# Tying the conversions of the later weight chunks to one another in VectorE's order

## The chip, the cores and the metric

The kernel runs on one core of a Trainium2 chip. The metric is the time of one execution in microseconds of the device; the kernel's time is the median of several executions. The core's engines named here are TensorE (PE in the rows; PEld is its weight load), VectorE (DVE), ScalarE (ACT), GpSimd (POOL) and SyncE (SP), which issues all of this kernel's DMAs. Each engine works through its own row of instructions in a fixed order; an instruction that waits for another engine or for a DMA holds up all behind it in its row.

## The reference

Windowed attention with a linear bias, followed by two feed-forward networks on the same 2304 tokens (4 x 576, 512 features as 8 heads of 64):

```python
scores = q @ k.T / sqrt(64) + slope[head] * -|i - j|   # only 0 <= i - j < 128
x = softmax(scores) @ v                                # 4 x 8 x 576 x 64 -> 2304 x 512
h = x @ w_in                                           # 512 -> 2048
x = (h * sigmoid(1.702 * h)) @ w_out                   # 2048 -> 512
g = x @ w_gate; val = x @ w_val                        # 512 -> 1536
out = (silu(g) * val) @ w_out2                         # 1536 -> 512
```

The inputs of the networks come as 64-bit floating-point words, which the kernel turns into pairs of 32-bit words itself.

## The kernel before

**Work.** The 2304 tokens are 18 tiles of 128, worked in five blocks of 4, 2, 4, 4 and 4 tiles (blocks 0 to 4). For each block attention makes the input x of the first network; the second network runs when all blocks are through the first. Every product of the first network is made as three matmuls, since each operand is a high and a low part: high x high (L554), high x low (L555), low x high (L556).

**Weights of the first network.** They come in 16 chunks. Chunk f is 128 of the 2048 hidden features: its part of w_in and its part of w_out, 512 KB each (`load_w`, L186). A chunk is converted in five steps (`split_steps`): L197 on ScalarE turns the upper words into a first value `cv`; L199 on VectorE shifts the lower words in place (`wraw`); L201 on VectorE puts both together in `cv`; L206 on ScalarE writes the high part of the weight `wt`; L208 on VectorE writes the low part. `cv` has two buffers, so two chunks can be under way. Chunks 0 to 7 are loaded at the start, 8 to 11 when the values of block 0 are made, 12 to 15 after that.

**Order.** The beginning is written out by hand: a table of tokens (`PLAN`) fixes the rows of TensorE, VectorE, ScalarE and GpSimd, with the attention of blocks 0 and 1 and the conversions of chunks 0 to 8 among it. Behind it a loop goes through pairs of block and chunk, `seq`: (0, 0..7), (1, 0..15), (0, 8..15), then (2, 0..15) and so on. For each pair `h_part` makes h = x @ w_in of the chunk, ScalarE and VectorE make its activation (th: L575 tanh on ScalarE, L577 on VectorE; gh: L583 on ScalarE; gl: L585 on VectorE), and two pairs later `y_part` multiplies it with w_out. Ahead of the products the loop calls `split_next` for the chunks that they need. In that part the rows of the engines are not fixed by hand: a scheduler places each instruction, by its own idea of when it can run, among the others, so that an instruction written late in the program can stand early in its engine's row.

**Attention.** Per pair of heads and tile: scores on TensorE (L354), masking (L317, L319, L324) and row minima (L379) on VectorE, exponentials and their sums on ScalarE (L395), reciprocals on VectorE (L407, L408), normalising on GpSimd (L414), transposes on TensorE (L446), values on TensorE (L507, L519), and the high and low parts of x, xh on ScalarE (L551) and xl on VectorE (L543).

**Names in the rows.** `wraw` is a raw chunk, `wt` a converted one, `sb` a bank of scores, `prob` and `stat` the probabilities and their row statistics, `hp` the bank of h, `y` that of the output, `wg` a weight tile of the second network. In the rows of the order the tiles have numbers: wraw_138 is chunk 2, 147 chunk 5, 548 to 557 chunks 8 to 11, 1044 chunk 13, 1050 chunk 15; wt_789 is chunk 4, wt_1037 chunk 8 and wt_1169 chunk 9.

Of the kernel before, what the change touches and what calls it, by code (L numbers as in the profile page):

```python
# [8 lines left out]
F32 = mybir.dt.float32  # L9
# [4 lines left out]
ALU = mybir.AluOpType  # L14
# [72 lines left out]
def attention_two_ffn(ctx: ExitStack, tc: tile.TileContext, q, k, v, w_in, w_out, w_gate, w_val, w_out2, yscr, wscr, woscr, out):  # L87
# [5 lines left out]
    nc = tc.nc  # L93
# [95 lines left out]
    def split_steps(raw):  # L189


        words, pool, tag = raw
        low, high = words[:, :, :, 0], words[:, :, :, 1]
        c = cvp.tile([P, 2, 512], U32, tag="cv", name="cv")
        cf = c.bitcast(F32)

        nc.scalar.activation(out=cf, in_=high.bitcast(F32), func=AF.Prelu, scale=REBIAS, alpha=NEGATIVE)  # L197
        yield
        nc.vector.tensor_scalar(out=low, in0=low, scalar1=29, scalar2=None, op0=ALU.logical_shift_right)  # L199
        yield  # L200
        nc.vector.scalar_tensor_tensor(  # L201
            out=c, in0=c, scalar=3, in1=low, op0=ALU.logical_shift_left, op1=ALU.bitwise_or
        )
        yield
        t = pool.tile([P, 2, 2, 512], F32R, tag=tag, name="wt")
        nc.scalar.activation(out=t[:, :, 0, :], in_=cf, func=AF.Copy)  # L206
        yield
        nc.vector.tensor_tensor(out=t[:, :, 1, :], in0=cf, in1=t[:, :, 0, :].bitcast(F32), op=ALU.subtract)  # L208
        yield [t[:, 0], t[:, 1]]

    def w1_src(i):
# [347 lines left out]
    marks = {}  # L559
# [292 lines left out]

    def split_next(w, raw, upto):
        for i in range(len(w), min(len(raw), upto)):
            w[i] = list(split_steps(raw[i]))[-1]

    for hp in range(H // 2):
        load_full(hp)
# [6 lines left out]
    def step(token):  # L865
# [10 lines left out]
        elif op == "N":  # L876
            reciprocals(*at)
        elif op == "P":
            normalise(*at)
        elif op == "T":  # L880
            transposes(*at, int(fills or 0))
        elif op in "CL":
            if op == "C" or at[0] or 2 * at[1] + at[2] not in ON_VECTOR:
                apart(*at, op == "L")
        elif op == "V":
            values(*at)
            valued[at[0]] += 1
            if at[0] == 1 and valued[1] <= H // 2 - 2:
                load_pair(1, valued[1] + 1)
            if at[0] == 0 and valued[0] == H // 2:  # L890
                load_w1(4)
        elif op in "XZ":
            take_x(*at, op == "Z")
        elif op in "Habcd":
            if op == "H":
                parts[at] = h_steps(*at)
            next(parts[at])
        elif op == "Y":
            y_part(*at)
        else:  # L900
            if op == "w0":
                splits[at] = split_steps(raw1[at[0]])
            done = next(splits[at])
            if op == "w4":
                w1[at[0]] = done
# [106 lines left out]
    for idx, (j, f) in enumerate(seq):  # L1012
# [4 lines left out]
        if j < 2:  # L1017
            need = f + 2
            if j == 1:
                need = max(need, F0 + (NF1 - F0) * (f + 1) // NF1)  # L1020
            split_next(w1, raw1, need)
# [109 lines left out]
```

## Time and profile before

| | us |
|---|---|
| runs | 931.45, 934.69, 935.67 (median 934.69) |
| the profiled execution, all of it | 936.22 |
| its span in the trace | 934.3 |
| TensorE busy | 904.1 |
| VectorE busy | 676.8 |
| ScalarE busy | 452.2 |
| GpSimd busy | 117.3 |

The span is from the first to the last recorded instruction; the execution has 1.9 us around it. The mean granted clock of TensorE is 0.989 of full speed. The rows further down are from this one execution. Such a row begins with the start and the duration; "[6.13 <-DMA ...]" at its end is the time for which the engine had stood idle before it, and what ended that.

### The profile page before, as it was taken

The page shows a single profiled execution, that of the slowest core. Times are in us where ns is not written, and L with a number is a line of the kernel's source. Part 1 is how long each engine was busy: PE and PEld are TensorE (multiplying, and loading weights), DVE is VectorE, ACT ScalarE, POOL GpSimd, SP SyncE. Part 2 cuts the span into 40 slices and gives each one's busy share as a digit, 9 for nine tenths or more (in the row PEclk, how much of TensorE's full clock was granted, in tenths as well). Part 3 has the DMA queues.
Part 4 walks back from the last instruction along what each step waited for, and adds up shares of the span by engine and source line. Part 5 has one row for each costly group of instructions (what it writes and reads, how often), then busy time and mean ns, then how long its engine had stood idle before and what let it go on. Part 6 is the DMA issues. An engine that isn't in the chain of part 4 may idle for free.

```text
span 934.3 us, 15603 instructions
## 1 busy us (share of the span) xinstructions
PE 904.1 (97%) x5572; PEld 801.1 (86%) x5572; DVE 676.8 (72%) x1716; ACT 452.2 (48%) x1052; POOL 117.3 (13%) x221
## 2 busy tenths in 40 slices
PE   6779999999999999999999999999999999999998
PEld 4456898777777877778888899999999999999998
DVE  7668685676676667766647668899976679866777
ACT  5645474554465446554434445545444435344331
POOL 4632102331233003230000000000000000000000
PEclk9979999999999999999999999999999999999999
DMA  9943311344654445434563587999897667887763
GB/s 327 343 178 105 119 47 34 115 159 140 217 196 161 155 173 186 139 125 174 201 234 114 214 325 282 319 351 340 323 342 283 247 238 242 281 298 249 262 243 136
DMA packets 72461, 201.30 MB, mean 215 GB/s; under 512 B 6848, under 2 KB 38080, under 8 KB 65472
## 3 DMA queue, kind: packets, MB, share of 16 engines
q1 hardware_dynamic: 72384, 200.31, 60.3%
q8 instruction: 44, 0.72, 0.3%
q14 instruction: 33, 0.27, 0.1%
HBM read 156.76 MB, written 43.52 MB: 214 GB/s over the span
## 4 chain that ended last, share of the span: by engine, by line
PE 87%; DMA 8%; DVE 2%; SPq 1%; ACT 1%; issue 0%; POOL 0%; DVEq 0%; ACTq 0%
PE sx L705 15%; PE ox L705 8%; PE sz L705 8%; PE hp L554 7%; PE y L554 7%; PE hp L556 7%; PE hp L555 7%; PE y L555 7%; PE y L556 6%; PE sy L705 4%; PE oz L705 4%; DMA wraw<-in_moe_w_out 4%; PE xb L507 2%; PE sb L354 2%; PE oy L705 2%; PE pt L446 1%
## 5 line engine op out<-in xcount | busy, mean ns | idle before, releaser
L705 PE MATMUL sx<-ya,wg 128*128 128x384 f32 x864 | 172.2, 336 | 1.2 <-DMA wg<-w_scratch 1.0
L705 PEld LDWEIGHTS sx<-ya,wg 128*128 128x128 f32 x864 | 151.6, 188 | 2.1 <-DMA wg<-w_scratch 2.0
L554 PE MATMUL hp<-xh,wt 128*128 128x512 f32 (+1 forms) x320 | 122.2, 382 | 1.5 <-DVE stat L379 1.4
L556 PE MATMUL hp<-xh,wt 128*128 128x512 f32 (+1 forms) x320 | 119.7, 374 | 0.3 <-DVE wt L208 0.3
L555 PE MATMUL hp<-xl,wt 128*128 128x512 f32 (+1 forms) x320 | 119.6, 374 | 0.0
L555 PE MATMUL y<-gl,wt 128*128 128x512 f32 (+1 forms) x320 | 117.9, 372 | 0.0
L556 PE MATMUL y<-gh,wt 128*128 128x512 f32 (+1 forms) x320 | 117.4, 371 | 0.0
L554 PE MATMUL y<-gh,wt 128*128 128x512 f32 (+1 forms) x320 | 113.6, 378 | 1.2 <-DVE yt L618 0.6
L414 POOL TENSOR_SCALAR prob<-prob,stat 128x128 f32<-128x128 f32 x144 | 67.6, 488 | 214.4 <-DVE stat L408 129.1
L585 DVE TENSOR_TENSOR gl<-th,gh 128x512 fp32r<-128x512 f32 (+1 forms) x80 | 51.9, 648 | 57.7 <-ACT gh L583 56.8
L705 PE MATMUL ox<-p,wg 128*128 128x384 f32 x432 | 89.7, 337 | 0.7 <-DMA wg<-wo_scratch 0.7
L705 PE MATMUL sz<-ya,wg 128*128 128x384 f32 x432 | 88.0, 336 | 0.0
L734 DVE TENSOR_TENSOR p<-th,p 128x384 fp32r<-128x384 f32 x126 | 68.2, 553 | 25.0 <-ACT p L733 24.2
L583 ACT ACTIVATE gh<-th 128x512 fp32r<-128x512 f32 (+1 forms) x80 | 46.8, 585 | 72.2 <-PE y L556 58.5
L733 ACT ACTIVATE p<-th 128x384 fp32r<-128x384 f32 x126 | 63.7, 521 | 35.1 <-DVE th L729 24.9
L705 PEld LDWEIGHTS ox<-p,wg 128*128 128x128 f32 x432 | 76.5, 188 | 1.0 <-DMA wg<-wo_scratch 1.0
L705 PEld LDWEIGHTS sz<-ya,wg 128*128 128x128 f32 x432 | 76.0, 188 | 0.1
L395 ACT ACTIVATE prob<-prob,stat 128x128 f32<-128x128 f32 x144 | 56.2, 392 | 39.4 <-DVE stat L379 39.4
L554 PEld LDWEIGHTS hp<-xh,wt 128*128 128x128 f32 x320 | 61.3, 192 | 14.5 <-issue 3.1
L556 PEld LDWEIGHTS hp<-xh,wt 128*128 128x128 f32 x320 | 61.3, 192 | 11.7 <-DVE wt L208 0.8
L554 PEld LDWEIGHTS y<-gh,wt 128*128 128x128 f32 x320 | 58.1, 188 | 15.0 <-issue 1.8
L555 PEld LDWEIGHTS hp<-xl,wt 128*128 128x128 f32 x320 | 61.4, 192 | 9.9
(94 smaller groups left out, 1535.9 us busy)
## 6 DMA issues: line engine op xcount, KB each, us to landing
wg<-w_scratch SPq DMA_DIRECT2D x36, 1024.0 KB, 5.2
wg<-w_scratch SPq DMA_DIRECT2D x36, 768.0 KB, 6.4
wg<-wo_scratch SPq DMA_DIRECT2D x18, 1024.0 KB, 6.4
wg<-wo_scratch SPq DMA_DIRECT2D x18, 768.0 KB, 8.1
w_scratch<-wa SPq DMA_DIRECT2D x24, 512.0 KB, 2.7
w_scratch<-wb SPq DMA_DIRECT2D x24, 384.0 KB, 3.2
wraw<-in_moe_w_in SPq DMA_DIRECT2D x16, 512.0 KB, 8.5
wraw<-in_moe_w_out SPq DMA_DIRECT2D x16, 512.0 KB, 8.8
```

What stands on the lines that cost most here:

```text
L354: nc.tensor.matmul(out=sb[e][c : c + size, (i % 2) * 256 + lo : (i % 2) * 256 + hi], lhsT=u["q"][rows, i * P + c : i * P + c + size], rhs= ...
L395: nc.scalar.activation(out=prob[:, x], in_=prob[:, x], func=AF.Exp, bias=stat[:, 0, x : x + 1], scale=-1.0, accum_out=stat[:, 1, x : x + 1],)
L414: (nc.vector if (j, hp, g) in NORM_ON_VECTOR else nc.gpsimd).tensor_scalar(out=prob[:, x], in0=prob[:, x], scalar1=stat[:, 3, x : x + 1], ...
L507: nc.tensor.matmul(out=x[r][e * D : (e + 1) * D, i * P + a : i * P + a + w], lhsT=u["v"][e][keys, kt + lead, :], rhs=u["pf"][keys].rearran ...
L554: nc.tensor.matmul(out=out_ap, lhsT=whi, rhs=xhi, start=start, stop=False)
L555: nc.tensor.matmul(out=out_ap, lhsT=whi, rhs=xlo, start=False, stop=False)
L556: nc.tensor.matmul(out=out_ap, lhsT=wlo, rhs=xhi, start=False, stop=stop)
L583: a = nc.scalar.activation(out=gh[:, :m], in_=th[:, :m], func=AF.Copy)
L585: d = nc.vector.tensor_tensor(out=gl[:, :m], in0=th[:, :m], in1=gh[:, :m].bitcast(F32), op=ALU.subtract)
L705: nc.tensor.matmul(out=bank_[:, :HT], lhsT=w[:, kk, at, a, :], rhs=p2[2 * (q // 2 - 1) + kk, i][:, b, :] if m == "O" else y2[q // NP2, i][ ...
L733: nc.scalar.activation(out=t[:, 0], in_=src, func=AF.Copy)
L734: nc.vector.tensor_tensor(out=t[:, 1], in0=src, in1=t[:, 0].bitcast(F32), op=ALU.subtract)
```

## The change

The low-part instruction L208 of each conversion is remembered as `marks["w"]`. In `split_next` a chunk's conversion is now built under `tc.issue_after(marks["w"])`: on VectorE, the engine of the marked instruction, the steps of this chunk come behind L208 of the chunk before it. ScalarE's order is not tied. No wait is added; only places in VectorE's row change, and with them what the scheduler puts around them. Chunks 0 to 8 in the table are as they were. In the changed kernel lines behind L208 have numbers higher by 2.

```diff
-        nc.vector.tensor_tensor(out=t[:, :, 1, :], in0=cf, in1=t[:, :, 0, :].bitcast(F32), op=ALU.subtract)
+        marks["w"] = nc.vector.tensor_tensor(
+            out=t[:, :, 1, :], in0=cf, in1=t[:, :, 0, :].bitcast(F32), op=ALU.subtract
+        ).ins
         yield [t[:, 0], t[:, 1]]
...
     def split_next(w, raw, upto):
         for i in range(len(w), min(len(raw), upto)):
-            w[i] = list(split_steps(raw[i]))[-1]
+            with tc.issue_after(marks["w"]):
+                w[i] = list(split_steps(raw[i]))[-1]
```

First place: VectorE's row before, where the last reciprocals of block 0 (stat_497) stand among conversions; wraw_138 and wraw_147 belong to the table.

```order
L199 TENSOR_SCALAR wraw_138<-wraw_138 128x1024
L199 TENSOR_SCALAR wraw_551<-wraw_551 128x1024
L407 TENSOR_SCALAR stat_497<-stat_497 128x4
L408 RECIPROCAL stat_497<-stat_497 128x4
L543 TENSOR_TENSOR xl_370<-xb_527,xh_369 128x512
L201 SCALAR_TENSOR_TENSOR cv_468<-cv_468,wraw_138 128x1024
L199 TENSOR_SCALAR wraw_147<-wraw_147 128x1024
L543 TENSOR_TENSOR xl_370<-xb_539,xh_369 128x512
L199 TENSOR_SCALAR wraw_557<-wraw_557 128x1024
L317 MEMSET sb_569 64x128
```

The same piece of VectorE's row now:

```order
L199 TENSOR_SCALAR wraw_138<-wraw_138 128x1024
L409 TENSOR_SCALAR stat_497<-stat_497 128x4
L410 RECIPROCAL stat_497<-stat_497 128x4
L545 TENSOR_TENSOR xl_370<-xb_527,xh_369 128x512
L201 SCALAR_TENSOR_TENSOR cv_468<-cv_468,wraw_138 128x1024
L199 TENSOR_SCALAR wraw_147<-wraw_147 128x1024
L545 TENSOR_TENSOR xl_370<-xb_539,xh_369 128x512
L319 MEMSET sb_569 64x128
```

The shifts of chunks 9 (wraw_551) and 11 (wraw_557) have gone from there to places further down.

Second place: VectorE's row before, where a score tile of block 1 (sb_764) is masked and its minima are taken, ahead of the low part of chunk 4.

```order
L324 COPY_PREDICATED sb_764<-later_72,sb_764 64x2x64
L199 TENSOR_SCALAR wraw_1044<-wraw_1044 128x1024
L379 ISA prob_791,stat_792<-sb_764,bias_71 128x128
L379 ISA stat_792 128x1
L379 ISA prob_791,stat_792<-sb_764,bias_71 128x128
L379 ISA stat_792 128x1
L208 TENSOR_TENSOR wt_789<-cv_690,wt_789 128x2x512
```

The same piece of VectorE's row now:

```order
L326 COPY_PREDICATED sb_764<-later_72,sb_764 64x2x64
L381 ISA prob_791,stat_792<-sb_764,bias_71 128x128
L381 ISA stat_792 128x1
L381 ISA prob_791,stat_792<-sb_764,bias_71 128x128
L381 ISA stat_792 128x1
L208 TENSOR_TENSOR wt_789<-cv_690,wt_789 128x2x512
```

The shift of chunk 13 (wraw_1044) has gone from between the mask and the minima.

Third place: VectorE's row before, at the first activations of block 1 (th_1066, th_1098), where steps of chunks 8, 9, 10 and 15 stand mixed.

```order
L199 TENSOR_SCALAR wraw_1050<-wraw_1050 128x1024
L201 SCALAR_TENSOR_TENSOR cv_1165<-cv_1165,wraw_551 128x1024
L585 TENSOR_TENSOR gl_1032<-th_1025,gh_1031 128x512
L199 TENSOR_SCALAR wraw_548<-wraw_548 128x1024
L577 SCALAR_TENSOR_TENSOR th_1066<-th_1066,hp_1053 128x256
L208 TENSOR_TENSOR wt_1169<-cv_1165,wt_1169 128x2x512
L201 SCALAR_TENSOR_TENSOR cv_1027<-cv_1027,wraw_548 128x1024
L577 SCALAR_TENSOR_TENSOR th_1098<-th_1098,hp_1085 128x256
L585 TENSOR_TENSOR gl_1070<-th_1066,gh_1069 128x256
L201 SCALAR_TENSOR_TENSOR cv_1236<-cv_1236,wraw_554 128x1024
L624 TENSOR_SCALAR yt_1117<-y_705 128x512
L208 TENSOR_TENSOR wt_1037<-cv_1027,wt_1037 128x2x512
```

The same piece of VectorE's row now:

```order
L199 TENSOR_SCALAR wraw_548<-wraw_548 128x1024
L579 SCALAR_TENSOR_TENSOR th_1066<-th_1066,hp_1053 128x256
L579 SCALAR_TENSOR_TENSOR th_1098<-th_1098,hp_1085 128x256
L201 SCALAR_TENSOR_TENSOR cv_1027<-cv_1027,wraw_548 128x1024
L587 TENSOR_TENSOR gl_1070<-th_1066,gh_1069 128x256
L208 TENSOR_TENSOR wt_1037<-cv_1027,wt_1037 128x2x512
L199 TENSOR_SCALAR wraw_551<-wraw_551 128x1024
L626 TENSOR_SCALAR yt_1117<-y_705 128x512
L201 SCALAR_TENSOR_TENSOR cv_1165<-cv_1165,wraw_551 128x1024
L587 TENSOR_TENSOR gl_1102<-th_1098,gh_1101 128x256
L579 SCALAR_TENSOR_TENSOR th_1142<-th_1142,hp_1129 128x256
L208 TENSOR_TENSOR wt_1169<-cv_1165,wt_1169 128x2x512
```

Chunk 8 is finished before chunk 9 begins, and so on to chunk 15, with th and gl of block 1 between the steps.

## Rows read from the trace of the kernel before

**Rows 1.** The page: busy time of the engines, and the chain that ended last

```profile
PE 904.1 (97%) x5572; PEld 801.1 (86%) x5572; DVE 676.8 (72%) x1716; ACT 452.2 (48%) x1052; POOL 117.3 (13%) x221
PE 87%; DMA 8%; DVE 2%; SPq 1%; ACT 1%; issue 0%; POOL 0%; DVEq 0%; ACTq 0%
```

**Rows 2.** TensorE's waits: us in total, times, longest us

```profile
PE pt L446 <- POOL prob L414: 8.7, 4, 6.5
...
PE sx L705 <- DMA wg<-w_scratch: 1.0, 1, 1.0
```

**Rows 3.** Windows: length, busy us of each engine (instructions), clock, DMA share, GB/s

```profile
56.00:72.00 16.00, 16.00 (x72) 12.58 (x72) 12.34 (x27) 9.96 (x20) 5.63 (x8) 0.88 0.23 79
...
90.00:107.00 17.00, 17.00 (x91) 13.14 (x91) 9.81 (x14) 5.73 (x9) 5.51 (x7) 1.00 0.30 106
107.00:136.00 29.00, 28.94 (x218) 27.69 (x217) 27.28 (x38) 23.66 (x36) 0.00 (x0) 1.00 0.19 71
136.00:180.00 44.00, 44.00 (x408) 38.14 (x409) 26.93 (x119) 22.60 (x78) 12.50 (x28) 1.00 0.17 54
```

**Rows 4.** What VectorE waited for ahead of L199: us, times

```profile
  DMA wraw<-in_moe_w_out: 13.4, 4
```

**Rows 5.** VectorE's timeline, 49 to 52 us

```profile
49.95 0.70 DVE L199 TENSOR_SCALAR wraw<-wraw 128x1024 uint32<-128x1024 uint32 x1 [6.13 <-DMA wraw<-in_moe_w_out]
50.56 0.16 DVE L407 TENSOR_SCALAR stat<-stat 128x4 f32<-128x4 f32 x1
...
51.43 1.22 DVE L201 SCALAR_TENSOR_TENSOR cv<-cv,wraw 128x1024 uint32<-128x1024 uint32 x1
```

**Rows 6.** Timelines of ScalarE and GpSimd, 43 to 53 us

```profile
43.72 0.19 ACT L395 ACTIVATION_READ_ACCUMULATOR prob<-prob,stat 128x1 f32 x1
...
52.68 1.06 ACT L206 ACTIVATE wt<-cv 128x1024 fp32r<-128x1024 f32 x1 [7.62 <-DVE cv L201]
...
51.13 3.48 POOL L414 TENSOR_SCALAR prob<-prob,stat 128x128 f32<-128x128 f32 x4 [9.59 <-DVE stat L408]
```

**Rows 7.** TensorE's timeline, 44 to 61 us

```profile
44.34 0.76 PE L354 MATMUL sb<-kr,qr 64*64 64x192 f32 x16
...
54.79 0.78 PE L554 MATMUL hp<-xh,wt 128*128 128x512 f32 x1
...
59.93 0.39 PE L554 MATMUL hp<-xh,wt 128*128 128x512 f32 x1
60.16 0.39 PE L555 MATMUL hp<-xl,wt 128*128 128x512 f32 x1
```

**Rows 8.** Timelines of VectorE and TensorE, 77 to 84 us

```profile
77.36 0.61 DVE L324 COPY_PREDICATED sb<-later,sb 128x128 f32<-128x128 uint32 x2
81.03 0.69 DVE L199 TENSOR_SCALAR wraw<-wraw 128x1024 uint32<-128x1024 uint32 x1 [3.05 <-DMA wraw<-in_moe_w_out]
...
82.28 0.47 PE L554 MATMUL hp<-xh,wt 128*128 128x512 f32 x1 [1.45 <-DVE stat L379]
...
83.33 0.56 PE L556 MATMUL hp<-xh,wt 128*128 128x512 f32 x1 [0.34 <-DVE wt L208]
```

**Rows 9.** Windows around the fall of the clock at 83.65 us, columns as in rows 3

```profile
80.23:83.65 3.42, 1.63 (x19) 0.94 (x16) 2.62 (x7) 1.22 (x5) 0.00 (x0) 1.00 0.91 320
83.65:87.06 3.41, 3.41 (x9) 2.64 (x8) 2.87 (x15) 2.11 (x6) 1.67 (x4) 0.50 0.05 18
```

**Rows 10.** SyncE's timeline, and the page's DMA issues (count, KB, us to landing)

```profile
49.84 0.33 SPq L302 DMA_DIRECT2D kr<-in_k  x1
...
kr<-in_k SPq DMA_DIRECT2D x4, 192.0 KB, 7.7
```

**Rows 11.** Timelines of VectorE at 112.53 us and of TensorE at 159.25 us

```profile
112.53 0.42 DVE L577 SCALAR_TENSOR_TENSOR th<-th,hp 128x256 f32<-128x256 f32 x1
...
159.25 0.28 PE L554 MATMUL hp<-xh,wt 128*128 128x256 f32 x1
```

## The prediction

> **What bounds the kernel now.** I read the page's first and fourth parts before anything else. TensorE is busy for 97% of the span, and the chain of work that ended last is 87% TensorE [rows 1]. So the time is TensorE's work plus the holes in it, and VectorE's conversions count only where TensorE stands for them. The next view is the list of what TensorE waited for. One entry is large: the transposes L446 waited 8.7 us for the normalised probabilities that GpSimd writes on L414, 6.5 us of it in one piece; a wait of a later stage, for a weight load, is 1.0 us [rows 2]. The windows by stage tell where TensorE has no hole at all: 56 to 72, 90 to 107 and 136 to 180 us are full, and 107 to 136 lacks 0.06 us [rows 3]. Whatever VectorE does in those stretches is worth nothing today. L199, the shift that the change holds back, sat four times behind a weight load that had not landed, 13.4 us in all [rows 4]. Two of the four, some 2.1 us each, lie in full stretches. The other two are 6.13 us ending at 49.95 and 3.05 us ending at 81.03 [rows 5, 8], and both lie where TensorE stands. The last thing I read is the clock: after each of the two holes the granted clock is at its lower level, 1.2 GHz, for some us, seen in matmuls whose starts lie 0.43 us apart instead of 0.23 [rows 7, 9].
>
> **The change, part by part.** It deletes and adds no instruction and no DMA. It changes which VectorE instructions stand behind which. ScalarE's L197 of the later chunks still goes early, GpSimd's row is the same, and on SyncE no load moves ahead of or behind a load that matters below.
>
> *First place, 44 to 55 us.* Today L199 of raw chunk 9 (wraw_551) stands in VectorE's row ahead of L407, the reciprocals for the last head pair of block 0, and waits for its load until 49.95. VectorE was free 6.13 us before that, at 43.82 [rows 5]. The sums that L407 needs were read by ScalarE by 43.72 + 0.19 = 43.91 [rows 6]. So L407, which started at 50.56, can start at about 43.95: **6.6 us earlier**. GpSimd's four L414, 3.48 us, wait for nothing else (9.59 us of idle time ended by L408) [rows 6]. TensorE is free from 44.34 + 0.76 = 45.10 [rows 7]. The first product of block 0, h(0,0), began at 54.79, right behind the last transpose, and also needs xl, whose two L543 stand behind L407 on VectorE and move with it. So it begins near 48.2. Bounds: 6.1, the wait alone, and 6.7, wait and instruction; I take 6.6.
>
> *The clock behind it.* The twelve products from 54.79 to 59.93 took 5.14 us, 0.43 each; from there they go at 60.16 - 59.93 = 0.23, twelve in 2.76 [rows 7]. With a hole of 3 us, in which the transposes run too, instead of one of 6.5 and some smaller ones, the clock may stay up: **2.4 us**. The lower bound is a clock that falls for as long as from 83.65 to 87.06 [rows 9]: eight products at 0.20 extra, 1.6, which leaves 0.7. I take 2.4, because TensorE is at work from the second us after 45.10 on.
> From 80.23 to 83.65 TensorE worked 1.63 of 3.42 us, and in the stretch after it the clock is 0.50 [rows 9]: it fell though the engine had not stood still. The Trainium skill, "TensorE: Matmul & The Clock Gate", Part 1 (The HAM clock gate), says that the gate judges recent activity in a rhythm that runs free of the kernel, so that the cost differs from run to run. One execution can't show that here. By that rule this gain could be there in one run and not in another, which is the third rival below.
>
> *Second place, 80 to 87 us.* L199 of chunk 13 (wraw_1044) stands between the masking of a score tile and its two minima L379. The masking was over at 77.36 + 0.61 = 77.97, the shift began at 81.03 [rows 8], and TensorE's next product, which takes over that tile's bank, stood 1.45 us. The lower half of its weight came late too: its L208 stands behind the minima, and the third product began at 83.33 where 82.28 + 0.46 was possible, about 0.5. Then the lower clock, 83.65 to 87.06 [rows 9], eight products at 0.20 extra: 1.6. Without the shift the minima start at 77.97 and L208 is over by about 79.8, ahead of 82.28 - 1.45 = 80.83, when TensorE is free. Gain 1.45 + 0.5 + 1.6 = **3.5 us**. The lower bound is 1.45, if the other two turn up elsewhere.
>
> *What is late next.* The loads of later scores: the last one is issued at 49.84 and takes 7.7 us by its group, so lands near 57.5 [rows 10]. SyncE issues it when it did. TensorE wanted it near 70 and will want it near 61, so it is still in time, by 3 us; a load that is 3 us later would be the new bound.
>
> *The tie itself, 107 to 160 us.* The seven chunks 9 to 15, and 8 ahead of them, can no longer overlap on VectorE. What queues behind a chunk's L208 is the next chunk's L199, and behind a waiting L208, which waits for ScalarE's L206, stand th and gl of block 1. Per chunk VectorE has 0.70 (L199) + 1.22 (L201) [rows 5] + 1.22 (L208, an estimate: one pass over a chunk as L201) + 4 x 0.42 (two th and two gl of block 1, [rows 11]) = 4.8 us. L206 between L201 and L208 takes 1.06 [rows 6], mostly covered by a th or gl; I add 0.3, and get 5.2, with bounds 4.8 and 5.9. Chunk 8's shift now stands right ahead of the first th of block 1, which began at 112.53, so the chain starts near 111.8. Eight chunks end at 111.8 + 41.6 = 153.4. The last one is wanted by h(1,15) at 159.25 [rows 11]: about 6 us in hand, and the earlier ones have more. **Cost 0**; the cover is gone at (159.4 - 111.8) / 8 = 5.95 us a chunk. VectorE is 94% busy there today (27.28 of 29.00 us) [rows 3] with the same work in it, so the hand is small but real.
>
> *The start of block 2, 136 to 180 us.* The last L208 moves into the first folds of block 2, and TensorE's row changes: up to 16 products of y that stood behind the first transposes of that block now stand ahead of them. At 44.00 us for 408 matmuls [rows 3], 0.11 each, these are 1.7 us of cover that is gone when the transposes' wait comes; with one L208 of 1.22 more in front of the folds, 2.9. Bounds 0 (something else is ready) and 3; I take **2.0** lost, nearer to the price of the products. The weight loads of the second network, which TensorE reaches 10 us earlier: 0 to 1.0, by the one wait there is [rows 2]; I take **0.5** lost.
>
> **Sum**: 6.6 + 2.4 + 3.5 - 2.0 - 0.5 = 10.0 us. The profiled execution took 936.22 us (span 934.3), 1.5 above the median of the runs, 934.69. So 936.2 - 10.0 = 926.2 for that one, and 934.7 - 10.0 = **924.7** for the median, 1.1% less.
>
> **Rivals.**
> *The tie costs more than the waits (slower).* If L208 waits for L206 in full at each chunk and th and gl come in the wrong place, so that a chunk takes 8 us and not 5.2, the eighth ends at 111.8 + 64 = 175.8, 16 late: 934.7 - 10.0 + 16 = 941. For it: VectorE's row is strict, and it is 94% busy. Against it: it needs 159.4 + 10 for nothing to be left, 57.6 / 8 = 7.2 us a chunk, above the bound of 5.9.
> *The wait only moves (same).* The first hole stays because something beside L407 holds TensorE until 54, for instance the load near 57.5 after all; then only the second place pays, less the 2.0 and 0.5 or so: 934.7 - 1 = 933.7. For it: the DMA engines are what made VectorE wait. Against it: GpSimd's idle time, the wait of the transposes and VectorE's wait end one behind the other within 2 us [rows 5, 6].
> *The clock falls again (less faster).* Both holes shrink, but the clock is low for eight products behind each: 924.7 + 1.7 + 1.6 = 928.0; behind one of them, about 926.4.
> *The change does nothing* (the shifts go as before in the first place) is excluded: the row of VectorE shows them gone from both places.
>
> **How the numbers follow.** Forecast with all gains, give or take the unknown ends: 0.55. The clock falls again: 0.20. The wait only moves: 0.17. Slower by the chain: 0.08. The predicted time is the forecast, 924.7. Its lower end takes the losses at 0 and the run-to-run spread of before: 921.5. The upper end takes both losses at their bounds (1.5 more), the clock behind both holes (3.3), and 1.5 for the spread: 931.0. A difference of 0.5%, 4.7 us, is about what a measurement of this kernel can tell from none; faster means below 930.0. That holds for the first two cases and a little of the third: 0.78. Same: 0.15, nearly all of the third. Slower: 0.07.
>
> **What would show it.** L407 starts at 44 to 45 us and GpSimd's L414 directly behind it; h(0,0) begins by 49; the products after it at 0.23 us if the clock holds, 0.43 if not. No wait of the minima L379 near 72 (the old 81). VectorE's L199 waits for a load nowhere. The last L208 ends 5 us or more before h(1,15). TensorE's waits between 136 and 180 come to under 3 us. The prediction is wrong if TensorE waits for L208 in block 1, if a load of scores becomes the releaser of TensorE between 55 and 70, or if TensorE's busy time in the full stretches changes.

## The result and the profile after

The changed kernel takes 926.06 us (median of 6 runs, 924.58 to 928.28); the kernel before, run beside it, 934.67 (931.45 to 935.67, 6 runs). The ratio is 0.9912, with a 95% interval from 0.9891 to 0.9933: 8.6 us or 0.9% faster, where 10.0 us were forecast. The profiled execution took 928.28 us, its span is 926.4; it is the slowest of the six, so the pair of profiles differs by 7.9 us.

First the page of the kernel after: busy time of the engines and the chain that ended last, the lines that answer to [rows 1].

```profile
PE 904.7 (98%) x5572; PEld 802.5 (87%) x5572; DVE 679.5 (73%) x1716; ACT 452.7 (49%) x1052; POOL 116.7 (13%) x221
...
PE 89%; DMA 4%; DVE 3%; ACT 1%; issue 1%; POOL 1%; SPq 0%; DVEq 0%; POOLq 0%; ACTq 0%
```

TensorE is busy as long as before (904.7 against 904.1 us) in a span that is 7.9 us shorter, so in this pair of profiles the difference is time in which TensorE stood. (What it gains by the clock behind the two holes it loses at other stretches of lower clock, which come further down.) The next view is TensorE's waits in the kernel after (us in total, times, longest), which answers to [rows 2].

```profile
PE sx L707 <- DMA wg<-w_scratch: 2.5, 2, 1.8
PE ox L707 <- DMA wg<-wo_scratch: 1.9, 1, 1.9
...
PE pt L448 <- POOL prob L416: 1.4, 2, 0.7
...
PE y L556 <- DVE stat L381: 1.0, 1, 1.0
PE hp L556 <- DVE stat L381: 0.5, 1, 0.5
```

The wait of the transposes for GpSimd has gone from 8.7 to 1.4 us. The waits for weight loads of the second network have grown, and two small ones for VectorE's minima are new. The kernel before had two small ones that [rows 2] leaves out, for a bank of y that had not been read out yet:

```profile
PE y L554 <- DVE yt L618: 0.6, 1, 0.6
PE y L554 <- ACT yt L622: 0.6, 1, 0.6
```

The first of them is 0.4 us in the kernel after, the second is gone. VectorE's L199 waits for no load any more; its 13.4 us [rows 4] are gone. The first place, in the timeline of VectorE (start, duration, then the instruction):

```profile
43.35 0.69 DVE L199 TENSOR_SCALAR wraw<-wraw 128x1024 uint32<-128x1024 uint32 x1
44.17 0.17 DVE L409 TENSOR_SCALAR stat<-stat 128x4 f32<-128x4 f32 x1
```

In that of GpSimd:

```profile
44.75 2.90 POOL L416 TENSOR_SCALAR prob<-prob,stat 128x128 f32<-128x128 f32 x4 [2.38 <-DVE stat L410]
```

And in that of TensorE:

```profile
45.82 0.76 PE L356 MATMUL sb<-kr,qr 64*64 64x192 f32 x16
...
47.71 0.33 PE L448 MATMUL pt<-ident,prob 128*128 128x128 f32 x1 [0.65 <-POOL prob L416]
47.79 0.48 PE L556 MATMUL hp<-xh,wt 128*128 128x512 f32 x1
48.11 0.39 PE L557 MATMUL hp<-xl,wt 128*128 128x512 f32 x1
48.34 0.39 PE L558 MATMUL hp<-xh,wt 128*128 128x512 f32 x1
```

The reciprocals start at 44.17 where they started at 50.56 [rows 5], and h(0,0) begins at 47.79 where it began at 54.79 [rows 7]. Its products start 0.23 us apart from the second one on, which is the 2.4 GHz level; the window (length, busy us of each engine, clock, DMA share, GB/s) says the same:

```profile
46.00:50.00 4.00, 3.35 (x30) 2.54 (x27) 3.50 (x12) 2.50 (x5) 2.84 (x3) 1.00 1.03 401
```

The second place, in TensorE's timeline:

```profile
70.79 0.76 PE L356 MATMUL sb<-kr,qr 64*64 64x192 f32 x16
71.48 0.50 PE L556 MATMUL hp<-xh,wt 128*128 128x512 f32 x1
71.82 0.40 PE L557 MATMUL hp<-xl,wt 128*128 128x512 f32 x1
72.05 0.39 PE L558 MATMUL hp<-xh,wt 128*128 128x512 f32 x1
72.28 0.39 PE L556 MATMUL hp<-xh,wt 128*128 128x512 f32 x1
```

The product that waited 1.45 us at 82.28 [rows 8] starts without a wait at 71.48, and none behind it is slow. The table follows the gain through the two profiles; h(0,2) is the product h of block 0 and chunk 2. Each line is the start of the same instruction of TensorE in both; the last column is what came with this line.

| | before | after | ahead | step |
|---|---|---|---|---|
| h(0,0) | 54.79 | 47.79 | 7.0 | +7.0 |
| h(0,2), clock up again in both | 63.8 | 54.5 | 9.3 | +2.3 |
| h(0,4), the second place | 82.28 | 71.48 | 10.8 | +1.5 |
| h(0,6) | 100.5 | 87.5 | 13.0 | +2.2 |
| h(1,0) | 107.19 | 94.22 | 13.0 | 0 |
| h(1,15) | 159.25 | 147.43 | 11.8 | -1.1 |
| first product of the second network | 530.6 | 518.6 | 12.0 | +0.2 |
| end of the span | 934.3 | 926.4 | 7.9 | -4.1 |

So 13 us were gained by 90 us, 1 was given back up to the second network, and 4 in it. The step of -1.1 at h(1,15) is for the most part no wait: between h(1,0) and h(1,15) TensorE's row has 191 products of y where it had 181, and the ten are missing behind h(1,15). What is lost between h(1,0) and the second network, 1.0 us, is about what the waits give: 0.38 for a gl of block 1 and 0.5 and 1.0 for the minima are new, and 0.8 of the waits for a bank of y is gone. The next section finds out which of these losses belong to the change.

### The profile page after: what moved, and what is told of

Same layout as the page of the kernel before. It is cut to its first block, busy times and chain, and to the rows that moved or that the text cites. A ratio compares the mean times of both kernels' runs of the same rounds, so it can differ in the third digit from the quotient of the medians.

```text
span 926.4 us, 15615 instructions
## 1 busy us (share of the span) xinstructions
PE 904.7 (98%) x5572; PEld 802.5 (87%) x5572; DVE 679.5 (73%) x1716; ACT 452.7 (49%) x1052; POOL 116.7 (13%) x221
## 4 chain that ended last, share of the span: by engine, by line
PE 89%; DMA 4%; DVE 3%; ACT 1%; issue 1%; POOL 1%; SPq 0%; DVEq 0%; POOLq 0%; ACTq 0%
PE sx L707 15%; PE ox L707 8%; PE sz L707 8%; PE hp L556 7%; PE y L556 7%; PE y L557 7%; PE hp L558 7%; PE hp L557 7%; PE y L558 7%; PE sy L707 4%; PE oz L707 4%; PE sb L356 2%; PE xb L509 2%; PE oy L707 2%; PE pt L448 1%; DMA wg<-wo_scratch 1%
## 5 line engine op out<-in xcount | busy, mean ns | idle before, releaser
L556 PE MATMUL hp<-xh,wt 128*128 128x512 f32 (+1 forms) x320 | 120.7, 377 | 0.5 <-DVE stat L381 0.5
L558 PE MATMUL hp<-xh,wt 128*128 128x512 f32 (+1 forms) x320 | 118.3, 370 | 0.0
L556 PEld LDWEIGHTS hp<-xh,wt 128*128 128x128 f32 x320 | 60.4, 189 | 13.3 <-issue 2.4
L556 PEld LDWEIGHTS y<-gh,wt 128*128 128x128 f32 x320 | 57.7, 188 | 14.6 <-issue 3.8
L557 PEld LDWEIGHTS y<-gl,wt 128*128 128x128 f32 x320 | 60.4, 189 | 11.1 <-issue 1.0
L558 PEld LDWEIGHTS y<-gh,wt 128*128 128x128 f32 x320 | 60.3, 188 | 11.1 <-issue 1.0
```

What stands on the lines that cost most here:

```text
L556: nc.tensor.matmul(out=out_ap, lhsT=whi, rhs=xhi, start=start, stop=False)
L557: nc.tensor.matmul(out=out_ap, lhsT=whi, rhs=xlo, start=False, stop=False)
L558: nc.tensor.matmul(out=out_ap, lhsT=wlo, rhs=xhi, start=False, stop=stop)
```

## Experiments

**Theory**: it was the early shift, an instruction that waited for its load at the head of VectorE's row, that cost the time; the tie pays by moving it, and costs nothing until the chain of conversions is too late for h(1,15). **Rivals**: the gain is the orderly sequence of the conversions; or a hole that is closed opens again at the next load.

**Leaving the shift out instead of tying.** Nothing is tied; the later chunks have no L199.

```diff
+        if shift:
             nc.vector.tensor_scalar(out=low, in0=low, scalar1=29, scalar2=None, op0=ALU.logical_shift_right)
...
-            out=c, in0=c, scalar=3, in1=low, op0=ALU.logical_shift_left, op1=ALU.bitwise_or
+            out=c, in0=c, scalar=3, in1=low, op0=ALU.logical_shift_left, op1=ALU.bitwise_or if shift else ALU.bitwise_and
...
-            w[i] = list(split_steps(raw[i]))[-1]
+            w[i] = list(split_steps(raw[i], False))[-1]
```

> The kernel before, nothing tied, but the shift L199 left out for chunks 9 to 15 (their low bits are masked in instead, so these weights are not the reference's). Theory (what cost time was the early shift that waits for its load, not the mixing of the chunks): both holes are gone as with the full change, h(0,0) at 48, h(1,0) at 94 to 95, and the time is 925 to 926 or up to 1 us less, since VectorE also has seven shifts of 0.7 us less. Rival (the orderly sequence of the chunks is what gains): 931 to 935.

Measured: 923.22 us, ratio 0.9887 (0.9867 to 0.9907). TensorE's timeline:

```profile
46.85 0.68 PE L447 MATMUL pt<-ident,prob 128*128 128x128 f32 x2 [1.50 <-POOL prob L415]
47.28 0.48 PE L555 MATMUL hp<-xh,wt 128*128 128x512 f32 x1
```

h(0,0) begins at 47.28 and h(1,0) at 93.7, as with the tie, with the conversions as mixed as before: up to the second network the rest of VectorE's row is that of the kernel before. The gain is the shift's place, not the sequence. The time is 0.8 us below the 924 to 926 of the theory. VectorE also has seven shifts, 4.8 us, less to do here, so this run alone doesn't say what the tie costs. Between 90 and 515 us TensorE has one wait of over 0.1 us here, 0.2 us.

**Tying only some of the chunks.** The same line, with a condition on the chunk:

```diff
-            with tc.issue_after(marks["w"]):
+            with tc.issue_after(marks["w"]) if i < 13 else ExitStack():
                 w[i] = list(split_steps(raw[i]))[-1]
```

(in the others `i >= 13` and `i < 11`.)

> Only chunks 9 to 12 are tied; 13 to 15 go as before, so the shift of chunk 13 still stands between the mask and the minima of the second place. Theory (two holes, each with its own price, the load of chunk 13 is issued behind loads that TensorE itself sets free and so moves with it): h(0,0) begins at 48 as with the full change, the wait at the second place is there again with TensorE standing about 1.4 us, h(1,0) begins near 98 instead of 94.2, and the time is about 3.7 us above that of the full change, 929 to 930. Rival (the load of chunk 13 lands at a fixed time near 81): the second hole grows by what the first one gave, to some 10 us, and the time is 934 to 935 as before.

> Only chunks 13 to 15 are tied; 9 to 12 go as before, so the shift of chunk 9 still stands ahead of the reciprocals. Theory: h(0,0) begins near 54.8 as before, the wait of the minima at the second place is gone with the lower clock behind it, h(1,0) begins near 103.5 instead of 107.2, and the time is 931 to 932. Rival (the second hole is only an echo of the first one): the second place stays as it was, no gain, 934 to 935.

Measured with 9 to 12 tied: 924.08 us, ratio 0.9894 (0.9874 to 0.9913), not the 929 to 930 of the theory. The theory's premise on the row was wrong. VectorE's timeline of this kernel at the second place:

```profile
68.16 1.22 DVE L208 TENSOR_TENSOR wt<-cv,wt 128x1024 fp32r<-128x1024 f32 x1
...
70.45 0.70 DVE L199 TENSOR_SCALAR wraw<-wraw 128x1024 uint32<-128x1024 uint32 x1 [0.47 <-DMA wraw<-in_moe_w_out]
```

Tying chunk 12 moved also the untied shift of chunk 13, behind the minima and behind L208 of chunk 4, where its wait of 0.47 us holds up nothing. The load of chunk 13 was there at 70.45, not at 81: it is issued behind loads for which TensorE has to set buffers free (SyncE issued it at 65.05 here, at 76.38 before), so a load may come earlier because the hole ahead of it was closed.

Measured with 13 to 15 tied: 931.99 us, ratio 0.9977 (0.9965 to 0.9989), inside the expected 931 to 932. h(1,0) is 5.9 us ahead, 2.0 of them at h(0,0) already: the load of chunk 9 landed at 47.99 in this execution, and still at the head of the row.

```profile
47.99 0.70 DVE L199 TENSOR_SCALAR wraw<-wraw 128x1024 uint32<-128x1024 uint32 x1 [4.46 <-DMA wraw<-in_moe_w_out]
```

The rest, 3.9, is the second place by itself. The second profile of the kernel before (further down) had the same early load; on that one this run is 0.1 us behind at h(0,0) and 3.8 ahead at h(1,0). What the first place gives alone was then looked at with only 9 and 10 tied, where the shift of chunk 13 stands between mask and minima again:

> Only chunks 9 and 10 are tied. VectorE's row then has the first place free (no shift of chunk 9 ahead of the reciprocals), and the shift of chunk 13 between the mask and the minima, as before the change. This is the experiment that the run with chunks 9 to 12 was meant to be. Theory (two holes of their own price; the load of chunk 13 follows a load that TensorE's values release, and so came 10 us earlier where TensorE was 10 us earlier): h(0,0) begins near 47.5; at the second place the shift waits some 3 us for its load, TensorE stands 1 to 2 us and has the lower clock behind it or not; h(1,0) begins at 95 to 97, and the time is 926 to 928, 2 to 3.5 us above the run with 9 to 12 tied. Rival (the second place costs nothing once TensorE comes there earlier): 924.

Measured: 928.84 us, ratio 0.9957 (0.9941 to 0.9973), above both. VectorE's timeline:

```profile
46.32 0.68 DVE L545 TENSOR_TENSOR xl<-xb,xh 128x512 fp32r<-128x512 f32 x1
51.03 0.69 DVE L199 TENSOR_SCALAR wraw<-wraw 128x1024 uint32<-128x1024 uint32 x1 [4.03 <-DMA wraw<-in_moe_w_out]
...
74.97 0.70 DVE L199 TENSOR_SCALAR wraw<-wraw 128x1024 uint32<-128x1024 uint32 x1 [2.48 <-DMA wraw<-in_moe_w_out]
```

TensorE's timeline, and two windows (length, busy us of each engine, clock, DMA share, GB/s):

```profile
56.23 0.50 PE L558 MATMUL hp<-xh,wt 128*128 128x512 f32 x1 [2.11 <-DVE wt L208]
...
76.23 0.47 PE L556 MATMUL hp<-xh,wt 128*128 128x512 f32 x1 [1.50 <-DVE stat L381]
```

```profile
54.00:58.00 4.00, 1.89 (x8) 1.46 (x8) 3.56 (x11) 2.81 (x9) 1.33 (x2) 0.96 0.75 243
58.00:62.00 4.00, 3.87 (x13) 2.74 (x13) 3.64 (x5) 3.58 (x6) 1.36 (x3) 0.62 0.17 71
```

h(0,0) begins at 46.7, 8.1 us ahead. But the shift of chunk 11, a few instructions further down (in the first place of the order above), now comes to its load 4.03 us early, and VectorE stands with the masks of the next scores and L208 of chunk 2 behind it: in h(0,2) TensorE waits 2.1 us for that L208, and the clock is at its lower level for a while after it. At the second place the theory held: the shift of chunk 13 waits 2.48 us and TensorE 1.5. Ahead by 10.4 us at h(0,2), the kernel is ahead by 6.1 at h(0,4) and at h(1,0), which begins at 101.1 and not at 95 to 97. In the kernel before the shift of chunk 11 had not waited, since the one of chunk 9 had used the time up. The rival of the moving wait is thus real: a hole closed alone opens at the next early shift, and the change gains because it takes these shifts away together.

**How much room the tie has.** L208 of each tied chunk is written twice, or three times:

```diff
         ).ins
+        for _ in range(again):
+            marks["w"] = nc.vector.tensor_tensor(
+                out=t[:, :, 1, :], in0=cf, in1=t[:, :, 0, :].bitcast(F32), op=ALU.subtract
+            ).ins
         yield [t[:, 0], t[:, 1]]
...
-                w[i] = list(split_steps(raw[i]))[-1]
+                w[i] = list(split_steps(raw[i], 1))[-1]
```

> The changed kernel with the low part L208 of each tied chunk (9 to 15) written twice, 1.22 us more on VectorE for each of seven chunks, 8.5 us in the chain. The chain as measured ends at 139.9 and h(1,15) begins at 147.4, so it has 7.5 us in hand. Theory (the chain is covered until that hand is used): 0 to 2 us over the changed kernel, 926 to 928. Rival (VectorE has no room there, each instruction shows): 8 us over it, 934.

> The same with L208 written three times, 2.44 us more for each of seven chunks, 17.1 us in the chain. Theory: 17.1 - 7.5 = 9.6 us over the changed kernel, 934 to 937. Rival (VectorE has no room there, each instruction shows): 17 us over it, 943. Rival (TensorE finds other work): under 3 us over it.

Measured: 929.87 us (ratio 0.9959, 0.9942 to 0.9975) and 935.63 (1.003, 1.0015 to 1.0045): about 4 and 10 us over the full change (925.7), or 5 and 12 by the ratios, since these runs and those of the full change were on different chips. In the changed kernel the chain looks so (VectorE, chunk 14's last step and chunk 15):

```profile
132.34 1.23 DVE L208 TENSOR_TENSOR wt<-cv,wt 128x1024 fp32r<-128x1024 f32 x1 [0.46 <-ACT wt L206]
133.49 0.69 DVE L199 TENSOR_SCALAR wraw<-wraw 128x1024 uint32<-128x1024 uint32 x1
...
138.72 1.22 DVE L208 TENSOR_TENSOR wt<-cv,wt 128x1024 fp32r<-128x1024 f32 x1
```

The shifts of chunks 8 and 15 start at 98.29 and 133.49, so a chunk takes 35.2 / 7 = 5.03 us. The last L208 is over at 139.94, 7.5 us ahead of h(1,15). From the L208 of chunk 9 to that of chunk 15 a chunk takes 5.25 us (107.23 to 138.72). With one L208 more these run from 106.25 to 148.91, 7.1 us a chunk: 1.22 us of work lengthened the cycle by 1.9. TensorE's timeline shows what is late then:

```profile
141.30 0.39 PE L560 MATMUL hp<-xh,wt 128*128 128x256 f32 x1 [0.98 <-ACT wt L206]
148.77 0.58 PE L560 MATMUL hp<-xh,wt 128*128 128x256 f32 x1 [1.97 <-ACT wt L206]
```

It is the high part of the weight, L206, in the last two chunks. ScalarE writes it, but ScalarE is not the cause: it had stood idle, and L206 starts 0.1 us behind the end of VectorE's L201, whose values it reads (last chunk; the row names the reciprocal L414, which VectorE runs right behind):

```profile
146.34 1.21 DVE L201 SCALAR_TENSOR_TENSOR cv<-cv,wraw 128x1024 uint32<-128x1024 uint32 x1
147.66 1.06 ACT L206 ACTIVATE wt<-cv 128x1024 fp32r<-128x1024 f32 x1 [0.38 <-DVE stat L414]
```

The windows from the shift of chunk 9 to that of chunk 15 show where the time goes (length, busy us of PE, PEld, DVE, ACT, POOL, then clock, DMA share, GB/s). The changed kernel:

```profile
103.68:133.49 29.81, 29.43 (x246) 28.76 (x245) 26.20 (x42) 20.54 (x35) 0.00 (x0) 1.00 0.10 37
```

With one L208 more, and its last 20 us:

```profile
102.71:144.83 42.12, 40.76 (x352) 38.65 (x351) 38.30 (x82) 26.29 (x56) 1.41 (x4) 1.00 0.12 40
130.00:150.00 20.00, 17.05 (x157) 14.69 (x159) 20.00 (x61) 13.11 (x36) 5.99 (x9) 0.97 0.09 31
```

The stretch is 12.3 us longer. Six L208 more are 7.3 of it, and 4.8 are other work of VectorE, 34 instructions more: th and gl, which go on coming from TensorE, and near the end the masks and minima of block 2. VectorE's idle time is nearly the same, 3.6 and 3.8 us, and in those last 20 us it has none. So the expectation of 0 to 2 us for one L208 more, which counted the added work alone, was too low. With two more, at 8.5 us a chunk, 9.6 were expected and 9.9 came; that is luck, for up to the last chunk's first L208 the chain had grown by 18.9 us and not by the 14.6 that were added, and h(1,15) needs L206 first, which stands ahead of L208. That a longer chain costs from some point on stands; the point is reached sooner than the added work says.

**What the second network takes back.** Three more profiles:

> The changed kernel once more, for a second profile. Its first profile was 12.0 us ahead of before at the first product of the second network and 7.9 at the end; 4 us went in waits for weight loads there (2.5 and 1.9 us) and a stretch at the lower clock. Theory (these waits belong to that execution): they are other ones this time, 1 to 3 us in sum, and the time is 924 to 927. Rival (the loads can't come 12 us earlier, so the gain is given back each time): the same waits with 4 us in sum again.

> The kernel before, once more, for a second profile. Theory (the two holes are in its order, not in one execution): TensorE's wait for the normalising 6 to 9 us in sum, VectorE's wait ahead of L199 12 to 14 us in four pieces, the wait of 1 to 2 us for the minima near 82, the lower clock behind both holes; h(1,0) at 106 to 108. What may differ is the second network's waits for weight loads, 1.7 us in the first profile, 1 to 4 us here.

> The full change on the same chip as the run with chunks 9 to 12 tied: 925 to 926. Waits of TensorE at the start of block 2 for the minima 0.5 and 1.0 us again (theory: they belong to the order); waits for weight loads of the second network 2 to 4 us, not the same ones (they belong to the execution).

Measured: the full change again 925.68 (0.9906, 0.9887 to 0.9924) and 925.33 (0.9907, 0.9892 to 0.9922). TensorE's waits of the first repeat:

```profile
PE sx L707 <- DMA wg<-w_scratch: 1.7, 2, 1.0
...
PE y L556 <- DVE stat L381: 1.0, 1, 1.0
...
PE ox L707 <- DMA wg<-wo_scratch: 1.0, 1, 1.0
PE sx L707 <- ACT pc L722: 0.8, 1, 0.8
PE hp L556 <- DVE stat L381: 0.5, 1, 0.5
```

The waits for minima (1.0 and 0.5 us, near 172 and 159 us) come again to the tenth in all three: they belong to the order. The waits for weight loads come again too, and not at other places, as was expected, but at the same three, with other lengths: some 19, 143 and 150 us behind the first product of the second network, 4.4 us in sum in the first profile, 2.7 and 2.5 in the two others. Of the three the kernel before has the first and the last in both of its profiles, 1.7 and 1.8 us in sum. Those of the second:

```profile
PE sx L705 <- DMA wg<-w_scratch: 1.2, 1, 1.2
PE ox L705 <- DMA wg<-wo_scratch: 0.6, 1, 0.6
```

The middle one, 0.6 to 0.8 us, came with the change in all three profiles, and the wait for ScalarE's pc, 0.8 and 0.7 us, in the two repeats. Why, no run shows. From the first product of the second network to the end the first profile of the change loses 4.1 us on that of before, the others 1.9 and 1.5, and the kernel before in its second profile loses 1.4 on its own first one. The mean of the two repeats is 1.0 us over the mean of the two profiles of before, so about 1 us of loss there comes with the change. In the first profile of the change the first of these waits was also followed by the lower clock (windows: length, busy us, clock, DMA share, GB/s):

```profile
533.00:537.00 4.00, 3.06 (x18) 2.74 (x16) 3.52 (x8) 1.49 (x4) 0.00 (x0) 1.00 1.02 426
537.00:541.00 4.00, 3.16 (x13) 3.17 (x14) 3.96 (x9) 1.89 (x5) 0.00 (x0) 0.77 1.00 409
541.00:545.00 4.00, 4.00 (x20) 4.00 (x20) 2.47 (x5) 2.26 (x6) 0.00 (x0) 0.80 0.14 58
```

In that of before the same stretch, 12 us later, has clock 1.00 throughout. So of the 4.1 us some 2.4 belong to that execution (4.1 less the mean of 1.9 and 1.5): longer waits and the lower clock. Of the rest 0.7 is that the first profile of before was better there than the mean of its two.

The second profile of before has both holes again, with 11.8 us of waiting ahead of L199 in four pieces, and the lower clock behind both. But the load of chunk 9 ended its wait at 47.84 instead of 49.95, and from there through block 1 this execution is 2.1 us ahead of the first one: h(1,0) begins at 105.1, under the 106 to 108 expected, and the 13.0 us of the table are 10.9 on this profile. The windows of 40 to 46 us differ in the clock. In its first profile:

```profile
40.00:46.00 6.00, 3.51 (x44) 2.35 (x44) 3.53 (x12) 3.09 (x7) 1.48 (x2) 1.00 0.97 331
```

In its second:

```profile
40.00:46.00 6.00, 5.04 (x44) 3.18 (x44) 2.89 (x11) 2.90 (x7) 0.20 (x1) 0.72 0.99 372
```

**A version with less of a tie.** With 9 to 12 tied the wait for gl is there but not the two for minima at the start of block 2, which are thus the price of tying 13 to 15. So it was run again beside the full change; and once with h(0,0) ahead of the transposes that still wait for GpSimd:

> Chunks 9 to 12 tied, again, on one chip with the full change. Theory (the ties of 13 to 15 give nothing and cost the waits of block 2's start, 0.49 + 1.04 us in both profiles of the full change, and what follows from that order): 1 to 2 us under the full change. Rival (the difference of 1.6 us between the two in the first comparison was chance): the same within 0.5 us.

```diff
-T:1.0.0 F0:1.1.0 H:0.0
+F0:1.1.0 H:0.0 T:1.0.0
```

> Chunks 9 to 12 tied, and in the table h(0,0) stands ahead of the transposes of block 1's first unit instead of behind them. Theory (what is left of the first hole is TensorE waiting for GpSimd's normalising, which h(0,0) doesn't need): h(0,0) begins 0.7 to 1.2 us earlier than with 9 to 12 tied alone, near 46, and the transposes fall behind it without a wait: 923. Rival (h(0,0) needs xl, whose second L545 ends only at 47 to 48, and the values of block 1 come later): no gain, 924 to 925.

Measured: 924.54 (0.9901, 0.9885 to 0.9918) against 925.33 for the full change on the same chip, between the 1 to 2 us of the theory and the 0.5 of the rival; the first pair was 924.08 against 925.68. At the first product of the second network it is 15.1 and 14.8 us ahead of before, the full change 12.0, 12.6 and 12.3. The profiles say about 2.5 us better, the times 0.8 to 1.6, and the intervals overlap: likely better, not settled. With h(0,0) moved: 923.31, ratio 0.9892 (0.9875 to 0.9909). h(0,0) begins at 43.89, earlier than expected, but stands 0.65 us for xl in its middle, and at h(1,0) only 0.5 us are left; against 0.9894 and 0.9901 that is no gain that can be told.

## Why the prediction was right, point by point

- **The first place** (6.6 forecast, 7.0 measured). The path was the one forecast: reciprocals, GpSimd, the last transpose, h(0,0). L407 at 43.95 forecast, 44.17 measured; h(0,0) at 48.2 forecast, 47.79 measured. What made it earlier is that GpSimd's four instructions took 2.90 us, not 3.48. TensorE came free at 46.58, not 45.10, since its clock was low ahead of it (0.72 in 40 to 46 us); that cost nothing, as the last transpose waited 0.65 us for GpSimd even so. The size hangs on when a load lands: on the second profile of before the gain is 4.9 us.
- **The clock behind it** (2.4 forecast, 0.7 as lower end; 2.3 measured). In all three profiles of the change the products of h(0,0) go at the higher level; the rival in which the clock falls again did not come up there. The clock was low elsewhere, ahead of the first place and once in the second network.
- **The second place** (3.5 forecast; 3.7 in the pair of profiles, 3.9 with 13 to 15 tied alone). Here the wait, the late L208 and the clock were all taken from rows, and all three went.
- **What is late next**: no load of scores became a releaser. The room was larger than the 3 us forecast: the scores that were made at 73.7 and 80.1 are made at 64.4 and 70.8 now, at least 7 us behind 57. What the prediction did not see is that the load of the next early shift would have been late next, if the tie had left that shift there (the run with 9 and 10 tied).
- **The tie** (cost 0, 5.2 us a chunk and 6 in hand forecast; 5.03 and 7.5 measured). One new wait of TensorE for gl, 0.38 us, is its trace in block 1. The prediction had ScalarE's L197 go as early as before; it waits 6.0 us in sum for L208 now instead of 3.5, and no wait of TensorE shows for it. The break-even of 5.95 us a chunk took VectorE's other work as fixed; the stretched chains show that a longer cycle takes in more of it.
- **The start of block 2** (2.0 lost forecast, within 0 to 3; 1.0 measured between h(1,0) and the second network). The part that was right: TensorE's row changed, more products of y stand early, and later TensorE has less to do while it waits for VectorE. But it waits 1.0 + 0.5 us for minima, at products that take over a bank of scores, and not at the transposes as forecast. The run without any tie and those with 9 to 12 tied have neither wait.
- **The second network** (0.5 lost forecast, 0 to 1.0; 4.1 in the pair of profiles, 1.9 and 1.5 in the two others). This is the term that was mis-sized. Its bound was the one wait in the profile of before; the change brought waits at places that had none, and executions of one kernel differ by more than that bound here.
- **Sum**: 7.0 + 2.3 + 3.7 - 1.0 - 4.1 = 7.9 us in the pair of profiles, 8.6 in the medians, against 10.0. The mean of the three profiles of the change against the mean of the two of before is 6.4 + 2.4 + 3.6 - 0.9 - 1.8 = 9.7; it is above the medians because the profiled executions of before were 1.5 and 1.9 us longer than their medians, those of the change 0.7 on average. So the gains were forecast well. That the two losses together came out near the forecast, 2.7 against 2.5, is luck: one was too high by 1.1 and the other too low by 1.3.

## What to carry to other kernels

An instruction that waits for a DMA at the head of an engine's row costs what stands behind it, so look at every wait of a side job (here a weight conversion) for a load, and ask who on the critical engine is behind it. Move all such instructions at once: with one gone the next one can meet its load earlier and take over the wait. Tie no more than needed, since a chain can lengthen by more than the work it is given: other work of the same engine comes in between (here 4.8 us beside 7.3 added).

## What was not expected of the hardware

The clock and the landing of a load differ between the two profiles of the kernel before at the same place: clock 1.00 or 0.72 in 40 to 46 us, and a load whose wait ended at 49.95 or 47.84. The Trainium skill, "TensorE: Matmul & The Clock Gate", Part 1 (The HAM clock gate), says that the number of products at the lower clock varies between runs of the same kernel. The two profiles agree, with the clocks just given. And four L414 on GpSimd took 3.48 and 1.67 us in the profile of before, 2.90 and 2.75 in that of after, for the same shape; no run here was made to tell why.
